# One array tile and one store for the output of a decode step: regrouping the last products of an attention-times-MLP kernel

## The chip, the cores and the metric

The kernel runs on one core of one Trainium2 chip. The metric is the device time of one execution in microseconds; lower is better. Three timed runs of the kernel before gave a median of 110.27 us. A profile comes from one further execution, whose own time is given beside its span below.

## What is computed

One decode step for two sequences (B = 2, one token each, D = 448): a layer-normed token attends to a cached window, the result goes through the output projection, and it is multiplied with a gate from a small MLP before the residual is added.

```
xn = layernorm(x)                                  # [2, 1, 448]
q  = (xn @ wq)                                     # 16 heads of 256
k, v = the last 2048 positions of the caches       # 8 KV heads, each serves 2 query heads
p  = softmax(q k^T / 16);  o = p v
s  = o.reshape(2, 1, 4096) @ wo                    # [2, 1, 448]
g  = silu(relu(xn @ w1) @ w2)                      # [2, 1, 448]
out = x + s * g
```

All inputs and the output are bf16. The output is 2 x 448 numbers.

## The kernel before, in words

**Staging.** Nearly all bytes are the K and V windows (2 x 8 heads x 2048 x 256, each 16 MB), beside wq, w1, w2 and wo. SP issues every load but x in one order: wq, w1, w2 (lines 259 to 261), four K blocks of 4 MB (one for each pair of sequence and half of the heads, line 263), then V into the same buffers kv[u] as the scores of block u are done with them (`load_v`, line 490), then wo in five parts of 20, 4, 5, 2 and 1 groups of 448 columns (`WO_PARTS`, line 166; issued at line 531). ACT issues the load of x and half of the output's store.

**Order of the work.** Each engine has a list of instructions written out by hand; `_Prog.run` emits it and puts a semaphore wait ahead of an instruction wherever a dependency is named. All products go through `mm` (line 312) and so have line 313 in the profile; all DMAs are line 39. An f32 product shows as two instructions in the profile. PE's list is laid out in blocks with branches that are never taken or always taken (`emit_pe`).

- Queries: seven products turn the normed token (L316), 28 make q (L338).
- `do_H` and `do_F` (lines 457 and 469) make the gate g. `do_H` uses 14 products of 448 columns with 128 weight columns on the whole array. `do_F` spreads 14 products over four array tiles, copies the four partial sums to zc, and adds them with four f32 products into mbk; ScalarE and VectorE then make silu from it (lines 483 to 487).
- For each of four blocks: VectorE turns K in place (`do_turn`, line 358), 32 products make scores (`do_S`), softmax (`do_max`, `do_et`), and later the products with V (`do_PV`).
- `fill` (line 417) issues f32 products of 512 columns with 8 weight columns whose result nobody reads.
- `do_turn_out` (line 446) turns the attention output into at2 with products of 64 columns; a VectorE copy at line 454 writes at2.
- Output projection (lines 536 to 561). The first 24 groups of wo are multiplied with two weight columns each, spread over four array tiles of wbk; VectorE copies them to wc in f32 (line 541). Then 40 products add everything into fbk: four f32 ones that sum the four partial sums in wc, and 32 bf16 ones for the last eight groups of wo.

**Array tiles and padded weights.** An array tile is named by `tile_position=(row, column)`; its column is also the partition at which the product's rows stand in the result. The 448 output columns are cut into four chunks of NCOL = 112, c = 0 to 3, and each product of the last stage serves one chunk. Chunk c = 2k + h goes to tile (0, 32h), so the result has its rows in partitions 0 to 3 (h = 0) and 32 to 35 (h = 1): ROWS = 36 partitions are handled, of which eight carry data. Within a tile, k chooses the row: the weights lie in buffers padded with zeros (at2 with PADW = 5 per group, fpad and xpad), and a window that starts at 1 - k puts the token's two columns in rows 2b + k and zeros in the other rows, so that all products of a tile can be added up in the same place. The tile of x itself (x_c, lines 328 to 335) and the gate are laid out in the same way. PSUM results of one tile are summed from `start` to `stop`.

**The end.** VectorE multiplies fbk with g (line 559), adds x_c (line 561), and SP and ACT each store four partitions of out_sb; SP waits for both.

```
d_o = [pr.dma(eng, half(out, h), out_sb[32 * h:32 * h + 4, :], [v_o]) for h, eng in ((0, SP), (1, ACTE))]
pr.op(SP, None, d_o)
```

The functions that the change touches follow.

Of the kernel before, what the change touches and what calls it, by code (L numbers as in the profile page):

```python
# [7 lines left out]
ACT = mybir.ActivationFunctionType  # L8
ALU = mybir.AluOpType
AX = mybir.AxisListType  # L10

PE, DVE, ACTE, SP, POOL = "pe", "dve", "act", "sp", "pool"
# [121 lines left out]
def bass_recurrent_scan__sliding_block_cached__dense_activation_relu__decode_kernel(  # L134
# [11 lines left out]
    B, Sq, D = A_x.shape  # L146
# [12 lines left out]
    HC = HD // 2  # L159
    FC = DFF // 2  # L160
    NCOL = D // 4
    ROWS = 36
    QC = 448
    XW = 160
    PADW = 5
    WO_PARTS = [20, 4, 5, 2, 1]
    WO_TILED = 24

# [1 line left out]
    with es:  # L170
        pr = _Prog(nc, es)
# [7 lines left out]
        def view(t, off, dims, n=128, p0=0):  # L179
            width = t.shape[1]  # L180
            return bass.AP(t, p0 * width + off, [[width, n]] + dims)
# [6 lines left out]
        wqo = named("wqo", [128, 32 * D], BF)  # L188
# [3 lines left out]
        ident = named("ident", [128, 128], BF)  # L192
# [6 lines left out]
        f8 = named("f8", [128, 8], F32)  # L199
        asel = named("asel", [128, 72], BF)  # L200
        x_sb = named("x_sb", [128, D], BF)
        x_c = named("x_c", [128, NCOL], BF)
# [11 lines left out]
        zc = named("zc", [128, D], F32)  # L214
        wc = named("wc", [128, D], F32)
        fpad = named("fpad", [128, PADW], F32)
        xpad = named("xpad", [128, PADW], BF)
        ea = named("ea", [128, NCOL], F32)
        g_sb = named("g_sb", [128, NCOL], F32)
        tmp = named("tmp", [128, NCOL], F32)  # L220
        out_sb = named("out_sb", [128, NCOL], BF)
# [11 lines left out]
        at2 = named("at2", [128, 32 * PADW], BF)  # L233

        sbk = [psum(f"sbk{i}", [128, 512], F32) for i in range(2)]
        obk = psum("obk", [128, 512], F32)
        spk = psum("spk", [128, 512], F32)
        mbk = psum("mbk", [128, 512], F32)
        qbk = psum("qbk", [128, 512], F32)
        wbk = psum("wbk", [128, 512], F32)  # L240
        fbk = psum("fbk", [128, 512], F32)

        def half(t, h):
            return t.rearrange("b s (k h n) -> h (b s k) n", h=2, n=NCOL)[h]

        def kv_src(u, cache):
            b, hg = divmod(u, 2)
            return cache[b, 4 * hg:4 * hg + 4, SK - W:SK, :].rearrange("g (p t) d -> p g (t d)", t=NT)

        d_x = pr.dma(ACTE, x_sb[0:B, :], A_x[:, 0, :])  # L250
        p_xc = pr.op(POOL, lambda e: e.memset(x_c[:, :], 0.0))
        wq_src = A_wq.rearrange("r (hf c) -> (r hf) c", hf=2).rearrange("(p s) c -> p (s c)", s=SLOTS)
        w1_src = B_w1.rearrange("r (hf c) -> (r hf) c", hf=2).rearrange("(p s) c -> p (s c)", s=SLOTS)
        w2_src = B_w2.rearrange("(p j) n -> p (j n)", j=14)
# [3 lines left out]
        st = {}  # L258
# [3 lines left out]
        for u in range(NU):  # L262
# [4 lines left out]
            out=ident[:, :], in_=ident[:, :], compare_op=ALU.not_equal, fill=1.0,  # L267
            base=0, pattern=[[-1, 128]], channel_multiplier=1), [i0])
        p_z = [pr.op(POOL, lambda e, t=t: e.memset(t[:, :], 0.0))
               for t in (fpad, xpad, asel, rm, bt, qstat, at2)][-1]  # L270
# [4 lines left out]
            out=sd[0:B, 0:1], in0=st2[0:B, 1:2], scalar1=EPS, scalar2=None, op0=ALU.add), [v_ag])  # L275
# [5 lines left out]
        def z(t):  # L281
            return a_z[t.name]
# [10 lines left out]
        v_pm = pr.op(DVE, red(pmask[:, :], view(ident, 0, [[1, 4], [4, 32]])))  # L293
        v_g8 = pr.op(DVE, red(view(g8, 0, [[2, 4], [1, 2]]), view(ident, 0, [[32, 4], [1, 2], [2, 4]])))
        v_f8 = pr.op(DVE, red(f8[:, :], view(ident, 0, [[1, 8], [8, 16]])))
        v_fp = pr.op(DVE, lambda e: e.tensor_copy(view(fpad, 1, [[2, B]]), f8[:, 0:B]), [v_f8, p_z])
        v_xp = pr.op(DVE, lambda e: e.tensor_copy(view(xpad, 1, [[2, B]], n=B), ident[0:B, 0:B]), [p_z])
        v_h2 = pr.op(DVE, red(half2[:, :], view(ident, 0, [[8, 2], [16, 8], [1, 8]]), AX.XY))
        v_gs = pr.op(DVE, lambda e: e.tensor_copy(
            view(gsum, 0, [[8, 16], [1, 8]]), view(g8, 0, [[0, 16], [1, 8]])), [v_g8])  # L300
# [4 lines left out]
        for e2 in range(2):  # L305
            v_xn = pr.op(DVE, lambda e, e2=e2: e.tensor_scalar(
                out=view(xg, 128 - 127 * e2, [[256, 4], [128, 2], [2, 64]], n=B),
                in0=view(x_sb, 3 * e2, [[1, 4], [0, 2], [SLOTS, 64]], n=B),
# [3 lines left out]
        def mm(out_ap, lhsT, rhs, start, stop=False, **kw):  # L312
            return lambda e: e.matmul(out_ap, lhsT=lhsT, rhs=rhs, start=start, stop=stop,  # L313
                                      skip_group_check=True, **kw)
# [12 lines left out]

        deps = [v_xp, d_x, z(sbk[1])]
        for c in range(4):
            k, h = divmod(c, 2)  # L330
            m_xc = pr.op(PE, mm(sbk[1][32 * h:32 * h + 4, 0:NCOL], xpad[0:B, 1 - k:5 - k],
                                x_sb[0:B, NCOL * c:NCOL * c + NCOL], k == 0, k == 1, tile_position=(0, 32 * h)), deps)
            deps = []
        d_xc = [pr.op(ACTE, lambda e, h=h: e.activation(
            x_c[32 * h:32 * h + 4, :], sbk[1][32 * h:32 * h + 4, 0:NCOL], ACT.Copy), [m_xc, p_xc]) for h in range(2)]

        deps = [d_wq, v_xr, z(qbk)]
        for s in range(SLOTS):  # L338
# [24 lines left out]

        def do_S(u):
            b, hg = divmod(u, 2)
            deps = [st["turn", u], st["q"], z(sbk[u % 2]), d_xc[1], st.get(("exp", u - 2))]
            for jp in range(8):
                j, par = divmod(jp, 2)
                for g in range(4):
                    o = pr.op(PE, mm(sbk[u % 2][32 * g:32 * g + 8, :],  # L370
                                     view(qstat, jp * 16 + 4 * g + 2 * hg + b, [[128, 8]]),
                                     view(kv[u], 64 * j + 2 * g + par, [[DH, NT], [8, 8]]),
                                     jp == 0, jp == 7, tile_position=(0, 32 * g)), deps)
                    deps = []
            last_S[u] = o
# [70 lines left out]
        def do_turn_out(hg):  # L446
            deps = [st["osb", 2 + hg], v_as, st["mbk"]]
            lo = 64 * hg
            for dq in range(8):
                o = pr.op(PE, mm(mbk[lo:lo + 64, 288:352], asel[:, 7 - dq:71 - dq],  # L450
                                 view(o_sb, hg * 2 * DH + 32 * dq, [[DH, B], [1, 32]]),
                                 dq == 0, dq == 7, tile_position=(0, lo)), deps)
                deps = []
            st["at"] = st["mbk"] = pr.op(DVE, lambda e: e.tensor_copy(
                view(at2, 1, [[2, B], [PADW, 32]], n=64, p0=lo), view(mbk, 288, [[32, B], [1, 32]], n=64, p0=lo)), [o, p_z])

        def do_H():
            deps = [st["w1"], v_xh, v_q]
# [10 lines left out]
        def do_F():  # L469
            deps = [st["w2"], st["h"], z(fbk)]  # L470
            for j in range(14):
                i = j % 4
                o = pr.op(PE, mm(fbk[32 * i:32 * i + B, 0:D], h_sb[:, 32 * j:32 * j + 2], w2_sb[:, j * D:j * D + D],
                                 j < 4, j >= 10, tile_position=(0, 32 * i)), deps)
                deps = []
            v = pr.op(DVE, lambda e: e.tensor_copy(zc[:, :], fbk[:, 0:D]), [o])
            deps = [v, v_fp, st["mbk"]]
            for c in range(4):
                k, h = divmod(c, 2)
                o = pr.op(PE, mm(mbk[32 * h:32 * h + 4, 0:NCOL], fpad[:, 1 - k:5 - k],  # L480
                                 zc[:, NCOL * c:NCOL * c + NCOL], k == 0, k == 1, tile_position=(0, 32 * h)), deps)
                deps = []
            a_e = pr.op(ACTE, lambda e: e.activation(ea[0:ROWS, :], mbk[0:ROWS, 0:NCOL], ACT.Exp, scale=-1.0), [o])
            v = pr.op(DVE, lambda e: e.tensor_scalar(
                out=ea[0:ROWS, :], in0=ea[0:ROWS, :], scalar1=1.0, scalar2=None, op0=ALU.add), [a_e])
            v = pr.op(DVE, lambda e: e.reciprocal(tmp[0:ROWS, :], ea[0:ROWS, :]), [v])
            st["g"] = st["mbk"] = pr.op(DVE, lambda e: e.tensor_tensor(
                out=g_sb[0:ROWS, :], in0=mbk[0:ROWS, 0:NCOL], in1=tmp[0:ROWS, :], op=ALU.mult), [v])

# [45 lines left out]
        deps = [st["at"], z(wbk)]  # L535
        for j in range(WO_TILED):
            i = j % 4
            o = pr.op(PE, mm(wbk[32 * i:32 * i + B, 0:D], view(at2, PADW * j + 1, [[2, B]]), wqo[:, j * D:j * D + D],
                             j < 4, j >= WO_TILED - 4, tile_position=(0, 32 * i)), deps + [landed.get(j)])
            deps = []  # L540
        v_wc = pr.op(DVE, lambda e: e.tensor_copy(wc[:, :], wbk[:, 0:D]), [o])  # L541
# [1 line left out]
        deps = [st["g"]]  # L543

        for c in range(4):
            k, h = divmod(c, 2)
            pr.op(PE, mm(fbk[32 * h:32 * h + 4, 0:NCOL], fpad[:, 1 - k:5 - k],
                         wc[:, NCOL * c:NCOL * c + NCOL], k == 0, tile_position=(0, 32 * h)), deps + [v_wc])
        for j in range(WO_TILED, 32):
            for c in range(4):  # L550
                k, h = divmod(c, 2)
                lo = j * D + c * NCOL
                m_o = pr.op(PE, mm(fbk[32 * h:32 * h + 4, 0:NCOL], at2[:, PADW * j + 1 - k:PADW * j + 5 - k],
                                   wqo[:, lo:lo + NCOL], False, j == 31,
                                   tile_position=(0, 32 * h)), deps + [landed.get(j)])
                deps = []

        pr.mark("dve_jump", eng=DVE)
        v_t = pr.op(DVE, lambda e: e.tensor_tensor(  # L559
            out=tmp[0:ROWS, :], in0=fbk[0:ROWS, 0:NCOL], in1=g_sb[0:ROWS, :], op=ALU.mult), [m_o, st["g"]])  # L560
        v_o = pr.op(DVE, lambda e: e.tensor_tensor(  # L561
            out=out_sb[0:ROWS, :], in0=tmp[0:ROWS, :], in1=x_c[0:ROWS, :], op=ALU.add), [v_t] + d_xc)
        d_o = [pr.dma(eng, half(out, h), out_sb[32 * h:32 * h + 4, :], [v_o]) for h, eng in ((0, SP), (1, ACTE))]
        pr.op(SP, None, d_o)
        pr.op(PE, None, [v_o])

        pr.run()
# [28 lines left out]
```

## Time and profile before

| | |
|---|---|
| three timed runs | 109.98, 110.27, 110.44 us (median 110.27) |
| profiled execution, its own time | 110.19 us |
| its span in the profile | 108.9 us |
| mean granted TensorE clock | 0.859 of full |
| PE busy, products | 60.8 us, 56% |
| VectorE busy | 62.3 us, 57% |
| ScalarE, GpSimd busy | 9.5 us, 2.2 us |
| read from HBM | 44.11 MB, 405 GB/s over the span |

The span runs from the first instruction to the last one of the core; all positions below are microseconds from its start. PE is TensorE's products, PEld its weight loads, DVE VectorE, ACT ScalarE, POOL GpSimd, SP SyncE; a q behind an engine's name is its sequencer, which issues DMAs. A row of the timeline gives start, length, engine, line, operation, result<-operands, their shapes, how many instructions are merged in it, and in brackets how long the engine was idle before it and what ended that. A merged row of n products that start evenly covers (n - 1) intervals and the length of the last one. The chain of waits is followed back from the last instruction: each piece is the work that released the next.

### The profile page before, as it was taken

To read this page: it belongs to the slowest core of one execution; us is meant where nothing else is said; L and a number is where in the kernel's file an instruction comes from. 1 tells how busy PE (TensorE), PEld (TensorE's weight loads), DVE (VectorE), ACT (ScalarE), POOL (GpSimd) and SP (SyncE) were. 2 spreads that over 40 slices of the span, in tenths; PEclk is the share of its full clock that TensorE was granted. 3 is DMA by queue.
4 is the path that set the end of the run, shared out by engine and by line. 5 is a ranking of instruction groups with operands and counts; after the bars stand their busy time and mean duration, and the time that the engine had idled before them with its cause. 6 is when DMAs were issued, how large, how long until landed. Compare 5 with 4: busy or idle time off the path is not lost.

```text
span 108.9 us, 1103 instructions
## 1 busy us (share of the span) xinstructions
PE 60.8 (56%) x459; PEld 16.4 (15%) x459; DVE 62.3 (57%) x87; ACT 9.5 (9%) x20; POOL 2.2 (2%) x14
## 2 busy tenths in 40 slices
PE   0002195943000069929961996299538966769672
PEld 0001023411000001101100220012023222303131
DVE  1933007344299979999999999940448332203021
ACT  4735000000000000002000200020020000000000
POOL 7000000000000000000000000000000000000000
PEclk9999999999655557995998599769965699999999
DMA  6899999999999999999999999999999899999960
GB/s 165 337 438 405 413 433 493 411 433 470 433 397 433 470 433 397 433 470 433 397 409 494 433 397 409 494 433 397 409 494 433 373 409 439 427 417 428 385 245 1
DMA packets 2471, 44.16 MB, mean 406 GB/s; under 512 B 290, under 2 KB 548, under 8 KB 804
## 3 DMA queue, kind: packets, MB, share of 16 engines
q1 hardware_dynamic: 2456, 44.11, 95.1%
q8 instruction: 3, 0.05, 0.2%
q10 hardware_dynamic: 12, 0.00, 0.0%
HBM read 44.11 MB, written 0.00 MB: 405 GB/s over the span
## 4 chain that ended last, share of the span: by engine, by line
DMA 55%; DVE 29%; PE 9%; SPq 4%; issue 1%
DMA kv<-in_A_k_cache_dram 33%; DVE kv L361 24%; DMA wqo<-in_A_wo_dram 22%; PE sbk L313 7%; SPq L39 4%; PE fbk L313 1%; PE wbk L313 1%; DVE q_x L390 1%; DVE rm L378 1%; DVE wc L541 1%; DVE rm_t L380 0%; DVE bias L384 0%; DVE bt L381 0%; DVE tmp L559 0%; DVE out_sb L561 0%
## 5 line engine op out<-in xcount | busy, mean ns | idle before, releaser
L313 PE MATMUL sbk<-kv,qstat 128*8 128x512 bf16 x128 | 30.0, 1091 | 21.3 <-DVE kv L361 21.3
L361 DVE STREAM_TRANSPOSE kv<-kv 128x2048 f32<-128x2048 f32 x16 | 35.6, 2275 | 3.0 <-DMA kv<-in_A_k_cache_dram 3.0
L313 PEld LDWEIGHTS sbk<-kv,qstat 128*8 128x8 bf16 x128 | 4.9, 107 | 44.9 <-DVE kv L361 27.2
L313 PE MATMUL obk<-kv,pt 128*16 128x512 bf16 x128 | 9.5, 441 | 2.5 <-DVE xg L442 1.2
L439 DVE TENSOR_SCALAR o_odd<-obk,rs 128x256 f32<-128x256 f32 x4 | 1.9, 484 | 11.1 <-PE obk L313 11.1
L385 ACT ACTIVATE e_sb<-sbk,bias 128x512 bf16<-128x512 f32 x4 | 2.7, 687 | 50.2 <-DVE bias L384 50.2
L313 PE MATMUL sbk<-kv,f 128*8 128x512 f32 x14 | 7.0, 620 | 0.0
L378 DVE TENSOR_REDUCE rm<-sbk 128x1 f32<-128x512 f32 x4 | 2.6, 662 | 4.8 <-PE sbk L313 4.8
L313 PE MATMUL qbk<-wqo,xr 128*4 128x512 bf16 x28 | 3.2, 626 | 3.9 <-DMA wqo<-in_A_wq_dram 3.9
L313 PE MATMUL mbk<-ident,xg 2*128 2x2 bf16 x7 | 0.3, 160 | 8.6 <-issue 8.6
L313 PEld LDWEIGHTS obk<-kv,pt 128*16 128x16 bf16 x128 | 3.2, 97 | 8.7 <-issue 5.0
L313 PE MATMUL qbk<-w_sb,xg 128*128 128x448 bf16 x14 | 4.4, 495 | 0.0
L344 DVE TENSOR_SCALAR q_x<-qbk 128x512 bf16<-128x512 f32 x1 | 0.7, 691 | 6.3 <-PE qbk L313 6.3
L390 DVE STREAM_TRANSPOSE q_x<-e_sb 128x512 bf16<-128x512 bf16 x4 | 2.8, 691 | 1.7 <-ACT e_sb L385 1.7
L407 DVE TENSOR_TENSOR pt<-spk,pmask 128x512 bf16<-128x512 f32 x4 | 2.6, 684 | 0.7 <-PE spk L313 0.7
L541 DVE COPY wc<-wbk 128x448 f32<-128x448 f32 x1 | 0.6, 624 | 3.8 <-PE wbk L313 3.8
L313 PE MATMUL spk<-q_x,perm 128*32 128x128 bf16 x16 | 0.6, 294 | 3.1 <-DVE q_x L390 3.1
L355 DVE CAST qstat<-mbk 32x256 bf16<-32x256 f32 x4 | 1.7, 421 | 0.7 <-PE mbk L313 0.7
L464 DVE TENSOR_SCALAR h_n<-qbk 128x448 bf16<-128x448 f32 x1 | 0.6, 623 | 2.6 <-PE qbk L313 2.6
L313 PEld LDWEIGHTS qbk<-w_sb,xg 128*128 128x128 bf16 x14 | 1.7, 130 | 2.3 <-issue 2.0
L442 DVE SCALAR_TENSOR_TENSOR xg<-obk,rs,o_odd 128x256 bf16<-128x256 f32 x4 | 1.9, 484 | 0.1
L272 DVE BATCH_NORM_STATS2 st<-x_sb 2x6 f32<-2x448 bf16 x1 | 0.6, 616 | 2.3 <-DMA x_sb<-in_A_x_dram 2.3
(79 smaller groups left out, 36.0 us busy)
## 6 DMA issues: line engine op xcount, KB each, us to landing
kv<-in_A_k_cache_dram SPq DMA_DIRECT2D x4, 4096.0 KB, 40.4
kv<-in_A_v_cache_dram SPq DMA_DIRECT2D x3, 4096.0 KB, 22.2
kv<-in_A_v_cache_dram SPq DMA_DIRECT2D x2, 2048.0 KB, 17.6
wqo<-in_A_wq_dram SPq DMA_DIRECT2D x1, 3584.0 KB, 12.3
w_sb<-in_B_w_dram SPq DMA_DIRECT2D x2, 1568.0 KB, 17.2
wqo<-in_A_wo_dram SPq DMA_DIRECT2D x1, 2240.0 KB, 24.4
wqo<-in_A_wo_dram SPq DMA_DIRECT2D x1, 560.0 KB, 25.8
wqo<-in_A_wo_dram SPq DMA_DIRECT2D x1, 448.0 KB, 24.8
```

Of the source, the lines that this page charges most:

```text
L39: o = _Op(eng, lambda e: e.dma_start(dst, src), [d for d in deps if d is not None], True)
L313: return lambda e: e.matmul(out_ap, lhsT=lhsT, rhs=rhs, start=start, stop=stop, skip_group_check=True, **kw)
L344: v_q = pr.op(DVE, lambda e: e.tensor_scalar(out=view(q_x, 0, [[256, 8], [128, 2], [1, 32]]), in0=view(qbk, 0, [[64, 8], [1, 2], [2, 32]]) ...
L355: st["q"] = st["mbk"] = pr.op(DVE, lambda e, Q=Q: e.tensor_copy(qstat[32 * Q:32 * Q + 32, 256 * Q:256 * Q + 256], mbk[32 * Q:32 * Q + 32, ...
L361: st["turn", u] = pr.op(DVE, lambda e, n=n: e.transpose(kf[:, 2048 * n:2048 * n + 2048], kf[:, 2048 * n:2048 * n + 2048]), [d_k[u]])
L378: v = pr.op(DVE, lambda e: e.tensor_reduce(out=rm[:, 0:1], in_=sbk[u % 2][:, :], axis=AX.X, op=ALU.max), [last_S[u], p_z, st.get(("rmt", u ...
L385: st["exp", u] = pr.op(ACTE, lambda e: e.activation(e_sb[:, :], sbk[u % 2][:, :], ACT.Exp, bias=bias[:, 0:1], accum_out=ssum[:, u:u + 1]), ...
L390: st["et", u] = pr.op(DVE, lambda e: e.transpose(q_x[:, 512 * u:512 * u + 512], e_sb[:, :]), [st["exp", u], m_qt])
L407: st["pt", u] = pr.op(DVE, lambda e: e.tensor_tensor(out=view(pt[u], 0, [[8, 64], [2, 4], [1, 2]]), in0=view(spk, 128 * u, [[2, 64], [0, 4 ...
L439: v = pr.op(DVE, lambda e: e.tensor_scalar(out=o_odd[:, :], in0=obk[:, DH:2 * DH], scalar1=rs[:, 2 * u + 1:2 * u + 2], scalar2=None, op0=A ...
L442: st["osb", u] = pr.op(DVE, lambda e: e.scalar_tensor_tensor(out=o_sb[:, lo:lo + DH], in0=obk[:, 0:DH], scalar=rs[:, 2 * u:2 * u + 1], in1 ...
L541: v_wc = pr.op(DVE, lambda e: e.tensor_copy(wc[:, :], wbk[:, 0:D]), [o])
```

## The change

- Chunk c of the output goes to row 4b + c. All four chunks of every such stage (x, the gate, the last 40 products) go to partitions 0 to 7 of one tile: no `tile_position` is given, the weights are 8 columns wide instead of 4, and the four chunks are summed in one place. ROWS is 8.
- The weight buffers are padded for this: PADW = 11, the token's columns stand four apart, and a window starts at 3 - c.
- x_c is written by one ScalarE activation of eight partitions instead of two of four, and GpSimd's memset of x_c is dropped.
- One SP store of eight partitions replaces the stores on SP and ACT. SP waits for one DMA.

The number of products and their columns stay. The diff, cut to its core:

```diff
-    ROWS = 36
+    ROWS = 8
-    PADW = 5
+    PADW = 11
...
-        p_xc = pr.op(POOL, lambda e: e.memset(x_c[:, :], 0.0))
...
-        v_fp = pr.op(DVE, lambda e: e.tensor_copy(view(fpad, 1, [[2, B]]), f8[:, 0:B]), [v_f8, p_z])
+        v_fp = pr.op(DVE, lambda e: e.tensor_copy(view(fpad, 3, [[4, B]]), f8[:, 0:B]), [v_f8, p_z])
...
         for c in range(4):
-            k, h = divmod(c, 2)
-            m_xc = pr.op(PE, mm(sbk[1][32 * h:32 * h + 4, 0:NCOL], xpad[0:B, 1 - k:5 - k],
-                                x_sb[0:B, NCOL * c:NCOL * c + NCOL], k == 0, k == 1, tile_position=(0, 32 * h)), deps)
+            m_xc = pr.op(PE, mm(sbk[1][0:ROWS, 0:NCOL], xpad[0:B, 3 - c:11 - c],
+                                x_sb[0:B, NCOL * c:NCOL * c + NCOL], c == 0, c == 3), deps)
             deps = []
-        d_xc = [pr.op(ACTE, lambda e, h=h: e.activation(
-            x_c[32 * h:32 * h + 4, :], sbk[1][32 * h:32 * h + 4, 0:NCOL], ACT.Copy), [m_xc, p_xc]) for h in range(2)]
+        d_xc = pr.op(ACTE, lambda e: e.activation(x_c[0:ROWS, :], sbk[1][0:ROWS, 0:NCOL], ACT.Copy), [m_xc])
...
-                view(at2, 1, [[2, B], [PADW, 32]], n=64, p0=lo), view(mbk, 288, [[32, B], [1, 32]], n=64, p0=lo)), [o, p_z])
+                view(at2, 3, [[4, B], [PADW, 32]], n=64, p0=lo), view(mbk, 288, [[32, B], [1, 32]], n=64, p0=lo)), [o, p_z])
...
             for c in range(4):
-                k, h = divmod(c, 2)
-                o = pr.op(PE, mm(mbk[32 * h:32 * h + 4, 0:NCOL], fpad[:, 1 - k:5 - k],
-                                 zc[:, NCOL * c:NCOL * c + NCOL], k == 0, k == 1, tile_position=(0, 32 * h)), deps)
+                o = pr.op(PE, mm(mbk[0:ROWS, 0:NCOL], fpad[:, 3 - c:11 - c],
+                                 zc[:, NCOL * c:NCOL * c + NCOL], c == 0, c == 3), deps)
...
         for c in range(4):
-            k, h = divmod(c, 2)
-            pr.op(PE, mm(fbk[32 * h:32 * h + 4, 0:NCOL], fpad[:, 1 - k:5 - k],
-                         wc[:, NCOL * c:NCOL * c + NCOL], k == 0, tile_position=(0, 32 * h)), deps + [v_wc])
+            pr.op(PE, mm(fbk[0:ROWS, 0:NCOL], fpad[:, 3 - c:11 - c],
+                         wc[:, NCOL * c:NCOL * c + NCOL], c == 0), deps + [v_wc])
         for j in range(WO_TILED, 32):
             for c in range(4):
-                k, h = divmod(c, 2)
                 lo = j * D + c * NCOL
-                m_o = pr.op(PE, mm(fbk[32 * h:32 * h + 4, 0:NCOL], at2[:, PADW * j + 1 - k:PADW * j + 5 - k],
-                                   wqo[:, lo:lo + NCOL], False, j == 31,
-                                   tile_position=(0, 32 * h)), deps + [landed.get(j)])
+                m_o = pr.op(PE, mm(fbk[0:ROWS, 0:NCOL], at2[:, PADW * j + 3 - c:PADW * j + 11 - c],
+                                   wqo[:, lo:lo + NCOL], False, j == 31), deps + [landed.get(j)])
...
-        d_o = [pr.dma(eng, half(out, h), out_sb[32 * h:32 * h + 4, :], [v_o]) for h, eng in ((0, SP), (1, ACTE))]
-        pr.op(SP, None, d_o)
+        d_o = pr.dma(SP, out.rearrange("b s (c n) -> (b s c) n", n=NCOL), out_sb[0:ROWS, :], [v_o])
+        pr.op(SP, None, [d_o])
```

More of the change, by code (lines that the diff above doesn't have):

```diff
@@ L241, in bass_recurrent_scan__sliding_block_cached__dense_activation_relu__decode_kernel @@
         fbk = psum("fbk", [128, 512], F32)
-        def half(t, h):
-            return t.rearrange("b s (k h n) -> h (b s k) n", h=2, n=NCOL)[h]
         def kv_src(u, cache):
@@ L295, in bass_recurrent_scan__sliding_block_cached__dense_activation_relu__decode_kernel @@
         v_f8 = pr.op(DVE, red(f8[:, :], view(ident, 0, [[1, 8], [8, 16]])))
-        v_fp = pr.op(DVE, lambda e: e.tensor_copy(view(fpad, 1, [[2, B]]), f8[:, 0:B]), [v_f8, p_z])
-        v_xp = pr.op(DVE, lambda e: e.tensor_copy(view(xpad, 1, [[2, B]], n=B), ident[0:B, 0:B]), [p_z])
+        v_fp = pr.op(DVE, lambda e: e.tensor_copy(view(fpad, 3, [[4, B]]), f8[:, 0:B]), [v_f8, p_z])
+        v_xp = pr.op(DVE, lambda e: e.tensor_copy(view(xpad, 3, [[4, B]], n=B), ident[0:B, 0:B]), [p_z])
         v_h2 = pr.op(DVE, red(half2[:, :], view(ident, 0, [[8, 2], [16, 8], [1, 8]]), AX.XY))
@@ L365, in do_S @@
             b, hg = divmod(u, 2)
-            deps = [st["turn", u], st["q"], z(sbk[u % 2]), d_xc[1], st.get(("exp", u - 2))]
+            deps = [st["turn", u], st["q"], z(sbk[u % 2]), d_xc, st.get(("exp", u - 2))]
             for jp in range(8):
@@ L537, in bass_recurrent_scan__sliding_block_cached__dense_activation_relu__decode_kernel @@
             i = j % 4
-            o = pr.op(PE, mm(wbk[32 * i:32 * i + B, 0:D], view(at2, PADW * j + 1, [[2, B]]), wqo[:, j * D:j * D + D],
+            o = pr.op(PE, mm(wbk[32 * i:32 * i + B, 0:D], view(at2, PADW * j + 3, [[4, B]]), wqo[:, j * D:j * D + D],
                              j < 4, j >= WO_TILED - 4, tile_position=(0, 32 * i)), deps + [landed.get(j)])
@@ L561, in bass_recurrent_scan__sliding_block_cached__dense_activation_relu__decode_kernel @@
         v_o = pr.op(DVE, lambda e: e.tensor_tensor(
-            out=out_sb[0:ROWS, :], in0=tmp[0:ROWS, :], in1=x_c[0:ROWS, :], op=ALU.add), [v_t] + d_xc)
-        d_o = [pr.dma(eng, half(out, h), out_sb[32 * h:32 * h + 4, :], [v_o]) for h, eng in ((0, SP), (1, ACTE))]
-        pr.op(SP, None, d_o)
+            out=out_sb[0:ROWS, :], in0=tmp[0:ROWS, :], in1=x_c[0:ROWS, :], op=ALU.add), [v_t, d_xc])
+        d_o = pr.dma(SP, out.rearrange("b s (c n) -> (b s c) n", n=NCOL), out_sb[0:ROWS, :], [v_o])
+        pr.op(SP, None, [d_o])
         pr.op(PE, None, [v_o])
```

## The prediction

> **What bounds the kernel now.** I read the page from the top: the span, the load of the DMA engines slice by slice, and the engine shares of the chain that ended last. Then I read that chain in order of time.
>
> ```profile
> span 108.9 us, 1103 instructions
> ...
> DMA  6899999999999999999999999999999899999960
> ...
> DMA 55%; DVE 29%; PE 9%; SPq 4%; issue 1%
> ```
>
> ```profile
> 78.86 24.37 DMA wqo<-in_A_wo_dram
> ...
> 103.36 1.38 PE wbk L313 x24
> 104.75 0.03 issue
> 104.77 0.63 DVE wc L541
> 105.41 0.04 issue
> 105.45 1.42 PE fbk L313 x40
> 106.87 0.02 issue
> 106.90 0.28 DVE tmp L559
> 107.17 0.02 issue
> 107.20 0.27 DVE out_sb L561
> ```
>
> The DMA engines are loaded from the second slice to the last but two, so up to 103.2 us the kernel runs at the pace of its loads, and what an engine gains or loses there is taken up by a wait for data. After that a chain with no gap wider than 0.04 us runs to the end: 24 products of the output projection, one copy, 40 products into fbk, two small VectorE operations, the store. Every nanosecond added or saved in this tail is one of the result. The change edits two of its links, the 40 products and the store.
>
> The profiled execution took 110.19 us, its span and 1.3 us around it. That is 0.08 below the median of the three runs, 110.27 (109.98 to 110.44). The sum below is made against 110.19.
>
> **The tail's products, which decide the sum.** The timeline of the tail, then a narrower window of it, the statistics of the two groups, and the stage's granted clock (the column before the DMA share):
>
> ```profile
> 105.45 0.56 PE L313 MATMUL fbk<-wc,fpad 128*4 128x112 f32 x8 [0.73 <-DVE wc L541]
> ...
> 105.84 1.02 PE L313 MATMUL fbk<-wqo,at 128*4 128x112 bf16 x32
> ```
> ```profile
> 105.84 0.66 PE L313 MATMUL fbk<-wqo,at 128*4 128x112 bf16 x20
> ```
> ```profile
> L313 PEld LDWEIGHTS fbk<-wqo,at x32: 80/85/86, 105.8 to 106.6; 128*4 128x4 bf16 x32
> L313 PE MATMUL fbk<-wqo,at x32: 211/212/213, 105.8 to 106.6; 128*4 128x112 bf16 x32
> ```
> ```profile
> 105.45:106.85 1.40, 1.40 (x40) 1.11 (x40) 0.00 (x0) 0.00 (x0) 0.00 (x0) 1.00 0.14 38
> ```
>
> The four f32 products appear as 8 instructions. They start at 105.45 and the first bf16 product starts at 105.84, so 8 instructions take 0.39 us of starts. They go to two array tiles (columns 0 and 32) in equal numbers: if the two run side by side, each tile takes 4 instructions in 0.386, 0.0965 each. Of the bf16 products the first 20 cover 0.66; less the 0.212 of the last one, that is 0.448 for ten per tile, so about 0.049 from one product of a tile to the next.
>
> After the change all 40 stand on one tile. What one tile can do is shown by streams that use one tile already: the filler products (f32, 512 columns, 8 weight columns), the products of do_H (bf16, 448 columns), and those of do_turn_out (bf16, 64 columns):
>
> ```profile
> 94.76 1.88 PE L313 MATMUL sbk<-kv,f 128*8 128x512 f32 x4
> ```
> ```profile
> 21.64 0.73 PE L313 MATMUL qbk<-w_sb,xg 128*128 128x448 bf16 x3
> ```
> ```profile
> 100.14 0.44 PE L313 MATMUL mbk<-xg,asel 128*64 128x64 bf16 x8 [0.27 <-DVE xg L442]
> ```
> ```profile
> L313 PE MATMUL sbk<-kv,f 128*8 128x512 f32 x7 | 3.5, 593 | 0.0
> ```
> ```profile
> L313 PEld LDWEIGHTS mbk<-xg,asel x16: 107/110/114, 93.1 to 100.4; 128*64 128x64 bf16 x16
> L313 PE MATMUL mbk<-xg,asel x16: 196/196/218, 93.1 to 100.4; 128*64 128x64 bf16 x16
> L313 PEld LDWEIGHTS qbk<-w_sb,xg x14: 97/151/151, 18.1 to 22.0; 128*128 128x128 bf16 x14
> L313 PE MATMUL qbk<-w_sb,xg x14: 352/568/581, 18.1 to 22.2; 128*128 128x448 bf16 x14
> ```
>
> The filler takes (1.88 - 0.593) / 3 = 0.429 per instruction, which for 112 columns in proportion is 0.094. do_H takes (0.73 - 0.352) / 2 = 0.189 for 448 columns, in proportion 0.047 for 112. do_turn_out takes (0.44 - 0.196) / 7 = 0.035 for 64; on the line between these two bf16 streams, 112 columns cost 0.054. The 0.0965 and 0.049 of the tail lie within a few per cent of what one tile does alone: in the old tail each tile already streams at its own full rate, and the pair gained a factor of two that the change gives back. I take 0.0965 and 0.049, the rows of the same shape, and keep 0.094 and 0.047 below, 0.100 and 0.054 above.
>
> From the first f32 start to the last bf16 start, before: 0.39 + (1.02 - 0.212) = 1.20. After: 8 x 0.0965 + 31 x 0.049 = 0.772 + 1.519 = 2.29. **The term is +1.09**, with bounds 0.75 + 1.46 - 1.20 = +1.01 and 0.80 + 1.67 - 1.20 = +1.27. The old 1.20 already holds what the last loads cost: its four last products start with a weight load of their own at 106.59.
>
> ```profile
> 106.59 0.09 PEld L313 LDWEIGHTS fbk<-wqo,at 128*4 128x4 bf16 x4
> ```
>
> In the new tail those products come at about 107.6, long after the data, so that wait disappears inside the longer stream; it is in the sum, since the old time contains it. The number of products, their columns and VectorE's two operations of 112 columns each (0.28 and 0.27 on the chain) stay.
>
> A rule speaks harder against the change. The Trainium skill (TensorE: Matmul & The Clock Gate, Part 3: Packing small matmuls, "What overlaps and what doesn't") says that a weight load overlaps a running product only where the two stand on other rows of the array. By it one tile would show each load. This trace does not agree: do_turn_out's loads last 110 ns on one tile and its products follow each other at 35 ns. The same page of the Trainium skill (Back-to-back issue gap) gives about 81 ns for a load and a product of 128 columns in a real kernel; an estimate from that page, 31 products at 81 ns, would make the term about +2.1 and the time about 112.2.
>
> **The store.** Two stores of four rows become one of eight on SP. The issue rows, what SP then waited, and the packets of 106 to 109 us in slices of 0.075 us:
>
> ```profile
> 107.49 0.35 SPq L39 DMA_DIRECT2D out_dram<-out_sb  x1
> 107.50 0.28 ACTq L39 DMA_DIRECT2D out_dram<-out_sb  x1
> ```
> ```profile
> SPq L69 <- DMA out_dram<-out_sb: 1.0, 1, 1.0
> ```
> ```profile
> GB/s 36 24 24 0 0 0 0 0 0 0 0 0 0 0 0 0 0 0 0 0 0 0 0 0 0 0 0 0 0 0 18 6 0 0 0 0 0 0 0 0
> ```
>
> Both issues start within 0.01 us of each other, so the second costs no time in line. Packets move only from 108.25 to 108.40; the rest of the 1.4 us is issue and completion, which don't depend on four rows or eight. SP's issue takes 0.07 longer than ACT's. From the last packet to the end of the span are 0.5 us, where the last load's packets (the third slice, to 106.22) released the PE at 106.59, 0.37 later. So a lone store could gain 0.13 there and 0.07 in the issue, 0.2 together. It could also lose: an SP issue of 128 partitions took up to 0.60 (the chain's piece at 78.21), 0.25 more than the 0.35.
>
> ```profile
> 78.21 0.60 SPq L39
> ```
>
> I take **-0.07**, ACT's issue price for a store without a companion that starts with it, and keep -0.2 and +0.25. The Trainium skill (DMA: Bandwidth & Descriptors, Queues, rings and completion order) says that a completion mark lands only after every earlier write of its DMA engine, from whichever queue; by that rule the companion's writes delay SP's mark and a lone store would gain, on the side of the -0.2. The trace shows no engine numbers with which to test it.
>
> **The other edits, at nothing.** The same regrouping lengthens the four f32 products of do_F, and the four of x on their way to x_c:
>
> ```profile
> 25.64 0.55 PE L313 MATMUL mbk<-zc,fpad 128*4 128x112 f32 x8 [0.72 <-DVE zc L476]
> ...
> 30.18 8.89 DVE L361 STREAM_TRANSPOSE kv<-kv 128x2048 f32<-128x2048 f32 x4 [2.26 <-DMA kv<-in_A_k_cache_dram]
> ```
> ```profile
> 9.27 0.53 ACT L334 ACTIVATE x_c<-sbk 4x112 bf16<-4x112 f32 x2 [2.91 <-PE sbk L313]
> ...
> 13.11 3.16 PE L313 MATMUL qbk<-wqo,xr 128*4 128x512 bf16 x28 [3.88 <-DMA wqo<-in_A_wq_dram]
> ```
>
> In do_F the price is again 0.39 us, and the gate's VectorE steps behind it shift by as much; VectorE then waits 2.26 us for the first K block, which covers it five times (uncovered, it would be +0.39). For x, four products on one tile cost 0.1 to 0.2 more and one activation of the two, half of 0.53, goes: both lie ahead of PE's 3.88 us wait for wq. POOL loses one memset and its last one covers 352 elements instead of 160, all before 4 us. The wider at2 changes the step of the copy at 100.61 us, not its 64x64 elements; its readers wait for wo until 103.36. No wait is added, and no queue is passed. SP's DMA order up to the store is as before; ACT's queue ends one store earlier, with nothing behind it.
>
> **Sum:** 110.19 + 1.09 - 0.07 = 111.21. Put on the median it would be 0.08 higher. I say 111.2.
>
> **The rivals.**
> *Weight loads show on one tile.* Then each product costs its load too: 8 x (0.0965 + 0.085) + 31 x (0.049 + 0.085) = 5.6 instead of 1.20, +4.4, 114.5 us; with half of each load shown, 112.9. For it: a stream of 112 columns is shorter than a load of 85 ns, and each load must be in flight before the one ahead has finished. Against: do_turn_out does that on one tile with even shorter products. Chance 0.08.
>
> *Not slower: the tail's pace is a shared one.* If 0.049 is what the sequencer needs for two loads and two products, about 12 ns each, and not the array's streaming time, one tile keeps the same pace per product: 1.20 stays, and the store makes it 110.1. It decides wherever one tile can take a 112-column bf16 product every 25 ns; up to that pace the last load at 106.59 holds the end. For it: four instructions fall into every 49 ns. Against: 64 columns on one tile already take 35 ns and 448 take 189, so the time follows columns. Chance 0.09.
>
> *The change gains in the store what nobody sees in the rows:* more than 0.55 net faster needs the store to be 1.6 us shorter, with the whole of it lasting 1.4. Together with a shared pace and a shift in the load stream, 0.03.
>
> **How the numbers follow.** The forecast has 0.80. Its ends: 110.19 + 1.01 - 0.2 = 111.0 and 110.19 + 1.27 + 0.25 = 111.7; the three runs spread by 0.2 below the profiled one, so the low end is 110.8. That range holds the 0.80 and needs none of the others. A measurement of this kernel can tell about 0.5%, 0.55 us, from no change: the forecast and the first rival lie above 110.82 (0.88, less 0.01 for the edge), the shared pace within (0.10), the last case below (0.03).
>
> **What would show it.** On the timeline of the changed kernel, right would be: the 8 f32 products start about 0.77 ahead of the first bf16 one instead of 0.39; the 32 bf16 products cover about 1.73 (31 x 0.049 + 0.212) instead of 1.02; the gaps ahead of the weight loads of the last two parts vanish; tmp starts near 108.0; one SP store of about 0.35 and a wait of about 1.0. If the 32 still cover about 1.0, the two tiles were never the reason and the shared pace holds. If they cover over 2.5, loads show. If the stream is as forecast and the time is not, it is the store, or a shift of the last load's landing.

## The result, and the profile after

The changed kernel took 111.28 us (median of 8 runs, 110.86 to 111.67), the kernel before 110.19 (8 runs, 109.98 to 110.78). The ratio is 1.0087, with a 95% interval of 1.0064 to 1.0110: slower by 0.96 us, 0.7 to 1.2 (the two medians are 1.09 apart). The forecast was +1.02 against its own profile. The profiled execution of the changed kernel took 111.49, its span 110.1.

First the page of the changed kernel, then its chain of waits from the last loads on:

```profile
span 110.1 us, 1099 instructions
...
DMA  6799999999999989999999999899989899999910
...
DMA 54%; DVE 28%; PE 10%; SPq 4%; issue 1%
```
```profile
79.17 24.29 DMA wqo<-in_A_wo_dram
103.46 0.14 issue
103.59 1.40 PE wbk L309 x21
104.99 0.02 issue
105.01 0.64 DVE wc L534
105.65 0.04 issue
105.69 2.52 PE fbk L309 x40
108.21 0.02 issue
108.24 0.27 DVE tmp L549
108.51 0.02 issue
108.53 0.26 DVE out_sb L551
```

The same chain with the same links, with other line numbers. One link has grown: fbk, 2.52 where it was 1.42. The copy wc starts 0.24 later, since the loads of wo landed later in this execution, and the two VectorE steps are as long as they were. From the issue of the store to the end of the span it is 1.25 (108.83 to 110.08) where it was 1.38 (107.49 to 108.87). So the two spans, 1.21 apart, differ by +0.24 ahead of the change, +1.10 in the products, -0.02 in VectorE and -0.13 in the store (0.02 is lost in rounding). The 0.24 doesn't belong to the change: in another kernel with the same products on one tile (the two-store experiment below), the same piece starts at

```profile
103.12 0.14 issue
103.26 1.40 PE wbk L309 x23
```

earlier than in the kernel before. The timeline of the changed tail, the statistics of its products, and the stage's row with the granted clock (1.00):

```profile
105.69 0.67 PEld L309 LDWEIGHTS fbk<-wc,fpad 128*8 128x8 f32 x8 [1.00 <-DVE wc L534]
105.69 0.94 PE L309 MATMUL fbk<-wc,fpad 128*8 128x112 f32 x8 [0.73 <-DVE wc L534]
106.37 1.66 PEld L309 LDWEIGHTS fbk<-wqo,at 128*8 128x8 bf16 x32
106.46 1.74 PE L309 MATMUL fbk<-wqo,at 128*8 128x112 bf16 x32
...
108.83 0.37 SPq L39 DMA_DIRECT2D out_dram<-out_sb  x1
```
```profile
L309 PEld LDWEIGHTS fbk<-wqo,at x32: 87/87/88, 106.4 to 107.9; 128*8 128x8 bf16 x32
L309 PE MATMUL fbk<-wqo,at x32: 212/213/213, 106.5 to 108.0; 128*8 128x112 bf16 x32
```
```profile
105.69:108.21 2.52, 2.51 (x40) 2.29 (x40) 0.00 (x0) 0.00 (x0) 0.00 (x0) 1.00 0.05 16
```

From the first f32 start to the first bf16 start 0.77 now pass (0.39 before), and 31 bf16 intervals take 1.74 - 0.213 = 1.53, 0.049 each. A weight load lasts 87 ns and is hidden all the same: the products follow each other at 49. In the window of the stage PE is busy 2.51 of 2.52, and no weight load waits for a landing any more.

### The profile page after: what moved, and what is told of

Read it like the earlier page. It is cut to its first block, busy times and chain, and to the rows that moved or that the text cites. A ratio compares the mean times of both kernels' runs of the same rounds, so it can differ in the third digit from the quotient of the medians.

```text
span 110.1 us, 1099 instructions
## 1 busy us (share of the span) xinstructions
PE 59.6 (54%) x459; PEld 17.4 (16%) x459; DVE 62.5 (57%) x87; ACT 9.2 (8%) x19; POOL 2.2 (2%) x13
## 4 chain that ended last, share of the span: by engine, by line
DMA 54%; DVE 28%; PE 10%; SPq 4%; issue 1%
DMA kv<-in_A_k_cache_dram 32%; DVE kv L355 24%; DMA wqo<-in_A_wo_dram 22%; PE sbk L309 7%; SPq L39 4%; PE fbk L309 2%; PE wbk L309 1%; DVE q_x L384 1%; DVE rm L372 1%; DVE wc L534 1%; DVE rm_t L374 0%; DVE bias L378 0%; DVE bt L375 0%; DVE tmp L549 0%; DVE out_sb L551 0%
## 5 line engine op out<-in xcount | busy, mean ns | idle before, releaser
L309 PE MATMUL obk<-kv,pt 128*16 128x512 bf16 x128 | 8.7, 414 | 3.5 <-DVE xg L436 1.6
L309 PE MATMUL qbk<-w_sb,xg 128*128 128x448 bf16 x14 | 2.8, 352 | 0.0
L309 PE MATMUL wbk<-wqo,at 128*2 128x448 bf16 x24 | 1.4, 352 | 1.0 <-DMA wqo<-in_A_wo_dram 1.0
```

## The experiments

The theory: the products of one array tile follow each other at their streaming time, two tiles stream side by side, and the change gave that up. Before, the tail's end was held by the last load, now it is held by PE. The lone store gives back about 0.1. Three rivals stand against it: a cost of the eight-row layout itself, a pace shared by all tiles, and a store whose number changes nothing. The timed runs of before beside the first four kernels have a median of 110.19 (18 runs), beside the last four 110.34 (23 runs).

### One tile in the old layout

Against the kernel before:

```diff
-            m_xc = pr.op(PE, mm(sbk[1][32 * h:32 * h + 4, 0:NCOL], xpad[0:B, 1 - k:5 - k],
-                                x_sb[0:B, NCOL * c:NCOL * c + NCOL], k == 0, k == 1, tile_position=(0, 32 * h)), deps)
+            m_xc = pr.op(PE, mm(sbk[1][0:ROWS, 0:NCOL], xpad[0:B, 33 - k - 32 * h:69 - k - 32 * h],
+                                x_sb[0:B, NCOL * c:NCOL * c + NCOL], c == 0, c == 3), deps)
...
-                m_o = pr.op(PE, mm(fbk[32 * h:32 * h + 4, 0:NCOL], at2[:, PADW * j + 1 - k:PADW * j + 5 - k],
-                                   wqo[:, lo:lo + NCOL], False, j == 31,
-                                   tile_position=(0, 32 * h)), deps + [landed.get(j)])
+                m_o = pr.op(PE, mm(fbk[0:ROWS, 0:NCOL], at2[:, PADW * j + 33 - k - 32 * h:PADW * j + 69 - k - 32 * h],
+                                   wqo[:, lo:lo + NCOL], False, j == 31), deps + [landed.get(j)])
```

(fpad, xpad and at2 are padded to match, PADW = 36; tmp shares ea's place to make room.)

> The layout of before (rows 0 to 3 and 32 to 35, two stores), but all 4-chunk products on one tile with weight windows of 36 columns. Theory (the lost overlap of two tiles is the whole cost of the products): 8 f32 products start over 0.77 us, 32 bf16 products cover 1.73, the fbk piece of the chain is 2.5 instead of 1.42, and the time is before plus 1.1, about 0.1 above the changed kernel, since the store is that of before. Rival (the eight-row layout or its weight windows cost it, not the tile): the fbk piece stays near 1.4 and the time at that of before.

Measured: 111.36 us, ratio 1.0106 (1.0075 to 1.0137). Its timeline:

```profile
105.54 0.96 PE L313 MATMUL fbk<-wc,fpad 128*36 128x112 f32 x8 [0.73 <-DVE wc L541]
106.24 1.67 PEld L313 LDWEIGHTS fbk<-wqo,at 128*36 128x36 bf16 x32
106.33 1.74 PE L313 MATMUL fbk<-wqo,at 128*36 128x112 bf16 x32
```

The f32 starts take 0.79 and the bf16 products the same 1.74, though the rows stand in 0 to 3 and 32 to 35 and a load brings 36 weight columns. The one tile alone brings the whole cost; rows, windows and store have no part in it.

### Four tiles

Against the kernel before:

```diff
-                m_o = pr.op(PE, mm(fbk[32 * h:32 * h + 4, 0:NCOL], at2[:, PADW * j + 1 - k:PADW * j + 5 - k],
+                m_o = pr.op(PE, mm(fbk[32 * c:32 * c + 2, 0:NCOL], at2[:, PADW * j:PADW * j + 2],
                                    wqo[:, lo:lo + NCOL], False, j == 31,
-                                   tile_position=(0, 32 * h)), deps + [landed.get(j)])
+                                   tile_position=(0, 32 * c)), deps + [landed.get(j)])
...
-        d_o = [pr.dma(eng, half(out, h), out_sb[32 * h:32 * h + 4, :], [v_o]) for h, eng in ((0, SP), (1, ACTE))]
+        d_o = [pr.dma(eng, out[b].rearrange("s (c n) -> (s c) n", n=NCOL),
+                      bass.AP(out_sb, b * NCOL, [[32 * NCOL, 4], [1, NCOL]]), [v_o]) for b, eng in ((0, SP), (1, ACTE))]
```

> Chunk c on array tile c, two weight columns, rows 32c and 32c+1, still two stores of four rows (one for each token, on SP and ACT). Theory (each tile streams on its own, and before was held at its end by the last load): the first f32 to the first bf16 start shrinks from 0.39 to about 0.19, four products start per 0.049 us, but the last part's four products still wait for its load; the fbk piece is 1.35 to 1.42 and the time that of before less 0 to 0.06. Rival (a pace shared by all tiles, 0.024 us per product): first f32 to first bf16 start stays 0.39, and the time too.

Measured: 110.93 us, ratio 1.0069 (1.0043 to 1.0094), slower where the theory said the same or a little less. Its timeline, and the chain of waits ahead of the end:

```profile
105.00 0.63 DVE L534 COPY wc<-wbk 128x448 f32<-128x448 f32 x1 [3.82 <-PE wbk L309]
...
105.68 0.37 PE L309 MATMUL fbk<-wc,fpad 128*2 128x112 f32 x8 [0.73 <-DVE wc L534]
106.00 0.24 PEld L309 LDWEIGHTS fbk<-wqo,at 128*2 128x2 bf16 x20 [0.21 <-DMA wqo<-in_A_wo_dram]
106.00 0.42 PE L309 MATMUL fbk<-wqo,at 128*2 128x112 bf16 x20
...
106.57 0.47 PE L309 MATMUL fbk<-wqo,at 128*2 128x112 bf16 x12 [0.15 <-DMA wqo<-in_A_wo_dram]
107.09 0.28 DVE L550 TENSOR_TENSOR tmp<-fbk,g_sb 98x112 f32<-98x112 f32 x1 [1.46 <-PE fbk L309]
...
107.70 0.65 SPq L39 DMA_DIRECT2D out_dram<-out_sb  x1
107.70 0.58 ACTq L39 DMA_DIRECT2D out_dram<-out_sb  x1
```
```profile
80.70 25.82 DMA wqo<-in_A_wo_dram
106.52 0.04 issue
106.57 0.50 PE fbk L309 x12
```

On the products it says what the theory said. 8 f32 instructions last 0.37 together where they took 0.56, 20 bf16 products 0.42: five on each tile at (0.42 - 0.21) / 4 = 0.05. A pace shared by all tiles is out. Data now hold the stage twice: the brackets have 0.21 ahead of the first 20 weight loads and 0.15 ahead of the last 12 products. So 0.32 pass from the first f32 start to the first bf16 start, not the 0.19 that was expected, and the chain now runs through the loads up to 106.52. From wc to tmp it is 2.09 where it was 2.13: twice the tiles gain 0.04, because the last load holds the end. The theory missed the store: its issue takes 0.65 and 0.58 instead of 0.35 and 0.28, and from the start of the issue to the end it is 1.92 instead of 1.38. That is 0.54 of the 0.74 lost in the medians, and within their interval (0.47 to 1.04) it is enough.

### The store split again

Against the changed kernel:

```diff
-        d_o = pr.dma(SP, out.rearrange("b s (c n) -> (b s c) n", n=NCOL), out_sb[0:ROWS, :], [v_o])
-        pr.op(SP, None, [d_o])
+        rows = out.rearrange("b s (c n) -> (b s c) n", n=NCOL)
+        d_o = [pr.dma(eng, rows[4 * h:4 * h + 4], out_sb[4 * h:4 * h + 4, :], [v_o]) for h, eng in ((0, SP), (1, ACTE))]
+        pr.op(SP, None, d_o)
```

> The changed kernel with its one SP store split again into two of four rows on SP and ACT. Theory (the lone store gains about 0.1 us, seen as 1.25 us from the store's issue to the end of the span instead of 1.38): 0.1 us slower than the changed kernel, with SP's wait and last step back at 1.38 us together. Rival (the store's number makes no difference, the 0.13 us between the two profiles is chance): the same time and about 1.25 us.

Measured: 111.33 us, ratio 1.0115 (1.0086 to 1.0143). From the issue at 108.49 to the end of its span it is 1.37. The timed runs can't tell 0.1 us: the interval overlaps that of the changed kernel. The profiles can: the four that store two groups of four neighbouring partitions (before, one tile in the old layout, this one and, below, before with half the products) take 1.37 or 1.38, the two with one SP store of neighbouring partitions (the changed kernel and, below, its half) 1.25.

### Four tiles with one store

Against the four-tile kernel; of the product's line only what changes is shown:

```diff
...
-                fbk[32 * c:32 * c + 2, 0:NCOL], at2[:, PADW * j:PADW * j + 2]
+                fbk[32 * c:32 * c + 17, 0:NCOL], at2[:, 32 * (j // 16) + j % 16:32 * (j // 16) + j % 16 + 17]
...
+        d_o = pr.dma(SP, out.rearrange("b s (c n) -> c (b s) n", n=NCOL),
+                     bass.AP(out_sb, 0, [[16 * NCOL, 8], [1, NCOL]]), [v_o])
```

> Four tiles, token b of chunk c in partition 32c+16b, weight windows of 17 columns, one SP store of eight partitions 16 apart. Theory: the products as in the four-tile kernel (fbk piece 1.35 to 1.42), the store as in the changed one (1.25 from its issue to the end): the time of before less 0.1 to 0.2. Rival (the lone store gains nothing): the time of before.

Measured: 110.64 us, ratio 1.0050 (1.0028 to 1.0072), slower where less than before was expected. The products take what they take in the four-tile kernel, the store's issue 0.69, and 1.74 pass from its start to the end. Both four-tile kernels lose at the store. In their stores, and in no other so far, the rows of one store don't lie in neighbouring partitions, and they lie in different quarters of the partitions. The experiment with a step of two, below, separates these.

```profile
107.42 0.69 SPq L39 DMA_DIRECT2D out_dram<-out_sb  x1
```

### Half the products, in both kernels

The edit in the changed kernel; in the kernel before the same two places change:

```diff
-        for j in range(WO_TILED, 32):
+        for j in range(28, 32):
...
-                                   wqo[:, lo:lo + NCOL], False, j == 31), deps + [landed.get(j)])
+                                   wqo[:, lo:lo + NCOL], False, j == 31), deps + [landed.get(24 if j == 28 else j)])
```

> The changed kernel without the 16 products of groups 24 to 27 (the output lacks their share). Theory (one tile: PE sets the end at 0.049 us per product): the fbk piece falls from 2.52 by 16 x 0.049 = 0.78 to about 1.74, and the time by 0.8, to about 0.3 above before. Rival (the end is set by the last load, as before): no change from the changed kernel.

> The kernel before without the same 16 products (the output lacks their share). Theory (two tiles: the last load sets the end, PE is idle in between): 8 pairs x 0.049 = 0.39 us of work go, but the last four products still start when their load has landed; the fbk piece loses 0 to 0.1 and the time stays at that of before. Rival (PE set the end before too, only faster): the time falls by 0.4.

Measured: the changed kernel without them 110.47 us, ratio to before 1.0010 (0.9996 to 1.0025); before without them 110.33, ratio 1.0013 (0.9996 to 1.0031). The first lies 0.13 above before in the medians, less than the 0.3 expected: on its chain fbk is 0.32 longer than before, and the lone store gives 0.13 back. The chain of the first and the timeline of the second:

```profile
105.22 1.74 PE fbk L309 x24
```
```profile
105.68 0.27 PE L313 MATMUL fbk<-wqo,at 128*4 128x112 bf16 x4
106.19 0.34 PEld L313 LDWEIGHTS fbk<-wqo,at 128*4 128x4 bf16 x12 [0.41 <-DMA wqo<-in_A_wo_dram]
106.19 0.52 PE L313 MATMUL fbk<-wqo,at 128*4 128x112 bf16 x12 [0.24 <-DMA wqo<-in_A_wo_dram]
106.75 0.27 DVE L559 TENSOR_TENSOR tmp<-fbk,g_sb 36x112 f32<-36x112 f32 x1 [1.51 <-PE fbk L313]
```

The same cut is worth 0.78 on the chain and about 0.9 us of time on one tile, each kernel taken against the runs of before beside it (0.85 by the ratios, 0.96 by the medians), and nothing on two, where a wait of 0.24 for the loads takes its place: from the start of fbk at 105.29 to tmp at 106.75 it is 1.46, as it was with all 40 products (1.45, 105.45 to 106.90). In the traces the last part of wo lands at 106.40 here and at 106.55 in the kernel before, and tmp starts 0.35 after it in both. With all 40 products the hold is slight: the last four start 0.11 after the ones ahead of them on their tiles instead of 0.05. This is the argument in one pair: in the kernel before the tail's products were free down to the last load's pace, in the changed one each costs its streaming time.

### Eight rows two partitions apart

Against the changed kernel:

```diff
-    ROWS = 8
-    PADW = 11
+    ROWS = 15
+    PADW = 21
...
-        d_o = pr.dma(SP, out.rearrange("b s (c n) -> (b s c) n", n=NCOL), out_sb[0:ROWS, :], [v_o])
+        d_o = pr.dma(SP, out.rearrange("b s (c n) -> (b s c) n", n=NCOL), bass.AP(out_sb, 0, [[2 * NCOL, 8], [1, NCOL]]), [v_o])
```

> The changed kernel with its eight rows in every second partition (0, 2 to 14): windows of 15 columns, 15 partitions handled, the same one SP store, now with a step of two partitions. Theory A (the four-tile kernels lost about 0.5 us because their stores step over partitions): SP's issue takes 0.65 to 0.7 instead of 0.37, issue to end of span 1.7 to 1.8 instead of 1.25, the time is 0.5 above the changed kernel. Theory B (they lost it because the rows lie in different quarters of the partitions): 0.37, 1.25 and the time of the changed kernel.

Measured: 111.83 us, ratio 1.0151 (1.0126 to 1.0177). The changed kernel had 1.0087 (1.0064 to 1.0110); each median less that of the runs of before beside it, the step costs 0.40. The store, and SP's wait behind it:

```profile
108.56 0.79 SPq L39 DMA_DIRECT2D out_dram<-out_sb  x1
```
```profile
SPq L69 <- DMA out_dram<-out_sb: 1.0, 1, 1.0
```

1.85 from the start of the issue to the end instead of 1.25, with all rows in one quarter of the partitions. Theory A holds and theory B is out: the step costs. Of the 0.59 more, 0.42 are in the issue (0.79 against 0.37) and 0.17 behind it (1.06 to the end against 0.89). The trace has 16 packets for this store as for the changed kernel's, so it isn't cut into more pieces. One rival is left: all the slow stores name their rows by an address pattern that is written out (`bass.AP`), and no run has neighbouring rows named in that way.

### The one store from ACT

Against the changed kernel:

```diff
-        d_o = pr.dma(SP, out.rearrange("b s (c n) -> (b s c) n", n=NCOL), out_sb[0:ROWS, :], [v_o])
+        d_o = pr.dma(ACTE, out.rearrange("b s (c n) -> (b s c) n", n=NCOL), out_sb[0:ROWS, :], [v_o])
```

> The changed kernel with its one store issued by ACT instead of SP; SP still waits for it. Theory (ACT issues the same store in less time, as the pair of before showed with 0.28 against 0.35): 0.07 us less from issue to end of span, 1.18 instead of 1.25, and the time 0 to 0.1 below the changed kernel. Rival (the issue time doesn't reach the landing): 1.25 and the same time.

Measured: 111.46 us, ratio 1.0117 (1.0090 to 1.0143). The issue takes 0.30, and 1.21 pass to the end, 0.04 less than from SP. The timed runs show no gain. Inconclusive between the two, and in any case too small to matter.

## Why the prediction was right, point by point

- **What bounds the kernel.** Right: the loads up to 103 us, then the tail. The half-product pair adds that in the kernel before PE had a little slack inside the tail: the last load, not the 40 products, set its end. So the prediction's sentence that every nanosecond added or saved in this tail is one of the result holds for the 1.1 added, and not for what is saved in the old products: 16 fewer saved nothing.
- **The tail's products, +1.09.** Right, by mechanism and size: 2.52 against 1.42, +1.10. The price per product, read off the old pairs as 0.0965 and 0.049, is that of the one tile (0.77 / 8 and 1.53 / 31). The single-tile streams of other shapes, used as a cross-check, were what made this more than a guess. One of them is misread, without effect on the term: the 35 ns of do_turn_out hold one longer first interval of 53, the others are 32.
- **The rule on weight loads.** The Trainium skill's sentence (TensorE: Matmul & The Clock Gate, Part 3) that a load overlaps a product only on other rows doesn't hold here: 87 ns loads on the same tile disappear behind products 49 ns apart. Nor did it hold in the kernel before, whose two tiles, (0, 0) and (0, 32), stand on the same rows: there 85 ns loads lay behind products 49 ns apart on each tile. The rival that loads show would have given 112.9 to 114.5 and is out. Out too are the 81 ns per pair that the same page of the Trainium skill gives for 128 columns: the 49 ns for 112 columns measured here are 56 in proportion.
- **The store, -0.07.** Right in sign, undersized, and for the wrong reason. The profile gives -0.13, and the interval of the timed runs is too wide to tell the two. I took it from the issue (ACT's price against SP's), but the lone SP issue takes 0.37, not less: eight rows take 0.02 more than four, on SP (0.37 against 0.35) as on ACT (0.30 against 0.28). What went is behind the issue, where the prediction's lower bound had a 0.13 too: 0.89 to the end of the span instead of 1.03. Most of that is SP's last step, which ends with the last mark (a mark is the semaphore increment that reports that data have landed): 17 ns instead of 183. The waits of 0.9 and 1.0 in the view run up to that last mark, so they contain the difference and don't come on top of it.

The changed kernel's wait and last step, then the last step of the kernel before:

```profile
SPq L69 <- DMA out_dram<-out_sb: 0.9, 1, 0.9
```
```profile
L69 SPq EVENT_SEMAPHORE  x1: 17/17/17, 110.1 to 110.1; - x1
```
```profile
L69 SPq EVENT_SEMAPHORE  x1: 183/183/183, 108.7 to 108.7; - x1
```

The two-store kernel has 1.37 again, with nothing else changed, so this is the companion's doing. In the trace the last packet of SP's store ends 0.87 us after its issue starts, with the companion as without. Counted from the same start, its marks come from 1.27 us on with the companion and from 1.14 on without, so the companion delays the marks and not the data. Through what, by the order of marks on shared DMA engines or otherwise, stays open: the trace doesn't number the engines.

- **The other edits, at nothing.** Right: in the changed kernel VectorE waits 3.68 us for the first K block after the gate, whose f32 products now last 0.93, and PE waits 4.14 us for wq.

```profile
24.10 0.93 PE L309 MATMUL mbk<-zc,fpad 128*8 128x112 f32 x8 [0.72 <-DVE zc L470]
...
30.41 2.31 DVE L355 STREAM_TRANSPOSE kv<-kv 128x2048 f32<-128x2048 f32 x1 [3.68 <-DMA kv<-in_A_k_cache_dram]
```
```profile
13.36 1.02 PE L309 MATMUL qbk<-wqo,xr 128*4 128x512 bf16 x8 [4.14 <-DMA wqo<-in_A_wq_dram]
```

- **The shared pace.** Out by the four tiles: four products start per 0.049 us, where a shared pace allows two.

None of these versions is faster than the kernel before. A store of neighbouring rows is 0.13 shorter with one issue, but here its rows come out of one tile, and that costs 1.1 in products; spread over four tiles, the rows lie apart and the store loses more than the tiles gain.

## What to carry to other kernels

Before putting small products on fewer array tiles, look at what follows them: where they end the kernel, the price is their streaming time (here 0.049 us for a bf16 product of 112 columns) times the number that used to run beside others. Whether that time was visible before is read from a wait for data ahead of the last products (in the kernel before a hold of 0.06 us that no bracket names), and tested by leaving half of them out. A saved DMA at the very end is worth about 0.13 us here, an eighth of what the layout for it cost.

## What the runs showed of the hardware that was not expected

A store whose rows lie in partitions with a step is slow to issue: SP takes 0.37 us for eight neighbouring partitions, 0.69 for a step of 16 and 0.79 for a step of 2; for four rows 0.35 against 0.65 at a step of 32. From the start of the issue to the end of the span this is 1.25 against 1.74 and 1.85, and 1.38 against 1.92. By the timed runs the step of 2 costs 0.40 us. All stepped stores here were named by a written-out address pattern, so it is not excluded that the pattern has a part in the cost.
